# Delaying four weight loads, shortening the warm-up, summing weights by halves and preparing tile 2 earlier at the start of a convolution and joint kernel

## The chip, the cores and the metric

The kernel runs on one core of one Trainium2 chip. The metric is the time of one execution on the device in microseconds (us). Runs of one kernel spread by about half a per cent, so each kernel below was run five or six times, in rounds that alternate with the kernel before on the same chip. A ratio is the mean time of one kernel's fast runs over the mean of the other's fast runs of the same rounds. A difference within 2% counts as "same"; everything here lies inside that band, and the questions are about half per cents. PE is the matrix engine, VectorE (DVE) and ScalarE (ACT) do elementwise work, and PSUM is the memory that PE writes its sums to, `acc` in the profile. A hole is a stretch in which PE has to wait between two matmuls.

## The reference

Two convolutions over time with five taps (zero padding of two, stride two, gelu after each), then a projection, a tanh joint with a second input, and an output projection. Cut to what matters:

```
x: (2, 4000, 512)   w1, w2: (5, 512, 512)   g: (2, 8, 512)   w_f, w_g, w_o: (512, 512)
h = gelu(sum_i xp[:, i:i+T, :] @ w1[i])[:, ::2, :]
f = gelu(sum_i hp[:, i:i+T1, :] @ w2[i])[:, ::2, :]
j = tanh((f @ w_f)[:, :, None, :] + (g @ w_g)[:, None, :, :])
return j @ w_o                                   # (2, 1000, 8, 512), bf16
```

## The kernel before

A convolution tile is not computed as ten products (five taps, two output phases) but as seven, by a fast-filter scheme. It needs differences of the four input phases, called a0, b1, b3, a3, a1, a2 (the function `xf`, on VectorE, some of them after a copy called `shift` on ScalarE). It also needs sums of weights: 2(w1+w3), w0+w4-w2 and w0+w4+w2. After the seven products a `post` puts them together: ScalarE copies one PSUM bank to `cs`, VectorE makes two scaled sums and a third, and ScalarE applies gelu.

The first tile of 254 columns (`t0`) is special, because at the start neither the weight sums nor the transposed input exist. Its input comes by two plain loads, 512 rows of x each (`xr`), and PE transposes them. Output blocks m = 0, 1 are computed directly from the plain taps, one tap at a time (`direct`); blocks 2, 3 by the filter (`filt`). Everything else of x comes by transposing DMAs. Warm-up matmuls on zeros fill PE until the samples are there.

The parts that the change touches, with cuts:

```
NWARM = 12
...
for rt in range(2):
    load_xr(rt)                          # two plain sample loads, 512 KB each
for i in (0, 1, 3, 4, 2):
    load_w1("sp", i)                     # five taps, 512 KB each, same queue
for ph in (2, 3, 1, 0):
    load_x(0, ph, 272, 528)              # transposing DMAs, same queue
...
warm_mm(NWARM)
for pp in range(2):                      # pp 0: phases 0, 2; pp 1: phases 1, 3
    for rt in range(2):                  # the two sample loads
        ...16 transposes in all per rt; copy pp 0 on VectorE, pp 1 on ScalarE
...
def wsum04(wsb, wt, eng, m):             # a quarter (128 columns of outputs) at a time
    tt(eng, s, wsb[0, :, sl], wsb[4, :, sl], add)          # f32
    tt(eng, wt[0, :, sl], s, wsb[2, :, sl], sub)
    tt(eng, wt[2, :, sl], s, wsb[2, :, sl], add)
...
def post(self, m, where, vec=(), scal=()):
    act(c, ps.cols(C, n), ACT.Copy, scale=0.5)             # cs
    flush()                              # the pending gelu of the post before
    for f in scal: f()                   # shifts of the next tile
    ...two scalar_tensor_tensor on VectorE...
    for f in vec: f()                    # xf of the next tile
    tt("dve", tv, tv, ps.pair(A, step, n), add)
    pending.append(lambda: self.gelu(m, tv))
...
for w in ("a0", "b1", "b3", "a1"): t1.xf(w)
wsum04(w1_sb, w1_t, "dve", 0)
t1.xf("a2"); t1.xf("a3")
wsum04(w1_sb, w1_t, "dve", 1)
for m, A in base0.items():
    t0.post(m, (A, A + NT, A + NT + 256, 256))
...
if qi == 1:                              # tile 1's posts prepare tile 2
    vec  = [... (), ("a0",), ("b1", "b3"), ("a1", "a2", "a3") ...][m]
    scal = [... ("a0",), ("b1",), (), ("a3",) ...][m]
```

## Time and profile before

| | before |
|---|---|
| median time | 281.73 us at the time of the prediction (three runs, 280.79 to 282.26) |
| profiled run | 282.13 us, span 280.3 us |
| PE busy | 98% |
| first real matmul | 8.99 us |
| last real matmul starts | 276.87 us |

The page's first part gives each engine's busy time, its share of the span and its instructions (kernel before):

```profile
PE 273.9 (98%) x1436; PEld 137.8 (49%) x1436; DVE 188.0 (67%) x250; ACT 160.3 (57%) x191; POOL 30.2 (11%) x39
```

A PE that is 98% busy seems to leave nothing to gain. But warm-ups count as busy too. The timeline of PE shows where its time is not the kernel's work. Its columns are start, length, engine, line, operation, tiles, shape, count and, in brackets, idle time before it with what ended it (kernel before):

```profile
1.29 4.86 PE L298 MATMUL acc<-zero 128*128 128x512 bf16 x12 [1.29 <-POOL warm L284]
...
8.99 5.39 PE L298 MATMUL acc<-xs_49,w_sb 128*128 128x254 bf16 x48 [1.05 <-DMA w_sb<-in_w_dram]
...
35.54 1.85 PE L298 MATMUL acc<-xt_55,w_sb 128*128 128x500 bf16 x8
37.38 1.02 PE L298 MATMUL acc<-xs_50,w_sb 128*128 128x500 bf16 x4
38.24 1.01 PE L298 MATMUL acc<-xs_50,w_t 128*128 128x500 bf16 x4
39.71 1.02 PE L298 MATMUL acc<-xt_55,w_t 128*128 128x500 bf16 x4 [0.47 <-DVE xt_55 L287]
40.95 1.02 PE L298 MATMUL acc<-xs_50,w_t 128*128 128x500 bf16 x4 [0.22 <-DVE xs_50 L287]
42.15 1.00 PE L298 MATMUL acc<-xt_55,w_sb 128*128 128x500 bf16 x4 [0.18 <-DVE xt_55 L287]
```

PE waits for the first tap of w1 before 8.99 us, and it waits three times for VectorE's `xf` results of tile 2 near 40 us. The chain of work that ended last (start, length, what), near those holes (kernel before):

```profile
39.69 1.20 DVE xs_50 L287
40.89 1.12 DVE xt_55 L287
42.02 0.14 issue
42.15 234.13 PE acc L298 x1112
```

From 42.15 to 276.28 us it is PE alone. Before that the chain does not run through PE at all: after the first loads it goes through VectorE, with some stretches of ScalarE. VectorE's timeline shows one long wait, and ScalarE's shows its reason (kernel before):

```profile
26.12 0.75 DVE L499 SCALAR_TENSOR_TENSOR ty_67<-acc,cs_65 128x254 f32<-128x254 f32 x2
...
31.80 0.74 DVE L499 SCALAR_TENSOR_TENSOR ty_67<-acc,cs_66 128x246 f32<-128x246 f32 x2 [1.42 <-ACT cs_66 L291]
...
40.81 1.20 DVE L287 TENSOR_TENSOR xt_55<-xt_55,xs_50 128x2000 bf16<-128x2000 bf16 x1
...
29.00 0.68 ACT L291 ACTIVATE hT_61<-ty_68 128x508 bf16<-128x508 f32 x1 [0.44 <-DVE ty_68 L287]
29.57 1.86 ACT L291 ACTIVATE xt_55<-xs_50 128x2000 bf16<-128x2000 bf16 x1
31.33 0.37 ACT L291 ACTIVATE cs_66<-acc 128x246 f32<-128x246 f32 x1
```

ScalarE runs in order. A gelu waits for VectorE, a 1.86 us shift stands behind the gelu, and the short `cs` copy that VectorE wants stands behind the shift.

### The profile page before, as it was taken

The page shows a single profiled execution, that of the slowest core. Times are in us where ns is not written, and L with a number is a line of the kernel's source. Part 1 is how long each engine was busy: PE and PEld are TensorE (multiplying, and loading weights), DVE is VectorE, ACT ScalarE, POOL GpSimd, SP SyncE. Part 2 cuts the span into 40 slices and gives each one's busy share as a digit, 9 for nine tenths or more (in the row PEclk, how much of TensorE's full clock was granted, in tenths as well). Part 3 has the DMA queues.
Part 4 walks back from the last instruction along what each step waited for, and adds up shares of the span by engine and source line. Part 5 has one row for each costly group of instructions (what it writes and reads, how often), then busy time and mean ns, then how long its engine had stood idle before and what let it go on. Part 6 is the DMA issues. An engine that isn't in the chain of part 4 may idle for free.

```text
span 280.3 us, 3870 instructions
## 1 busy us (share of the span) xinstructions
PE 273.9 (98%) x1436; PEld 137.8 (49%) x1436; DVE 188.0 (67%) x250; ACT 160.3 (57%) x191; POOL 30.2 (11%) x39
## 2 busy tenths in 40 slices
PE   8899989999999999999999999999999999999995
PEld 3799934444444444444444444444444444444442
DVE  0989797956896766686424363676776775666764
ACT  2533949328426533932336565948957957966930
POOL 1000000099992000000000000000000000000000
PEclk9999999999999999999999999999999999999999
DMA  7999999990000000000000020444454445444444
GB/s 251 291 179 201 213 211 191 316 325 3 4 0 0 2 0 0 0 2 0 0 0 4 0 75 5 155 155 154 135 169 151 150 144 170 145 155 145 155 150 140
DMA packets 54719, 31.85 MB, mean 114 GB/s; under 512 B 31646, under 2 KB 54446, under 8 KB 54702
## 3 DMA queue, kind: packets, MB, share of 16 engines
q1 hardware_dynamic: 54702, 31.62, 41.8%
q8 instruction: 11, 0.18, 0.3%
q14 instruction: 6, 0.05, 0.1%
HBM read 7.86 MB, written 16.38 MB: 87 GB/s over the span
## 4 chain that ended last, share of the span: by engine, by line
PE 84%; SPq 6%; DVE 5%; issue 2%; ACT 1%; DMA 1%; DVEq 0%
PE acc L298 84%; SPq L330 4%; SPq L316 2%; DMA xs_49<-in_x_dram 1%; ACT xt_55 L291 1%; DVE xs_50 L287 1%; DVE xt_55 L287 1%; DVE w_t L287 1%; DVE ty_68 L499 1%; DVE ty_68 L287 0%; DVE xt_54 L287 0%; SPq L321 0%; DVE ty_67 L499 0%; DVE ty_69 L499 0%; DVE ssum_71 L287 0%
## 5 line engine op out<-in xcount | busy, mean ns | idle before, releaser
L298 PE MATMUL acc<-wo_sb,jT 128*128 128x512 bf16 (+1 forms) x504 | 108.3, 378 | 0.0
L298 PEld LDWEIGHTS acc<-wo_sb,jT 128*128 128x128 bf16 x504 | 49.3, 98 | 58.8
L298 PE MATMUL acc<-xt_55,w_sb 128*128 128x500 bf16 (+1 forms) x192 | 42.1, 357 | 0.2 <-DVE xt_55 L287 0.2
L291 ACT ACTIVATE jT<-feT_80,geT 128x1000 bf16<-128x1000 f32 (+6 forms) x44 | 35.8, 889 | 0.0
L291 ACT ACTIVATE jT<-feT_79,geT 128x1000 bf16<-128x1000 f32 (+4 forms) x40 | 35.1, 948 | 0.0
L298 PE MATMUL acc<-xt_54,w_sb 128*128 128x500 bf16 (+1 forms) x160 | 33.2, 342 | 0.0
L298 PEld LDWEIGHTS acc<-xt_55,w_sb 128*128 128x128 bf16 x192 | 18.6, 98 | 18.7 <-issue 0.9
L291 ACT ACTIVATE cs_65<-acc 128x500 f32<-128x500 f32 (+2 forms) x13 | 7.0, 538 | 27.3 <-PE acc L298 27.3
L298 PEld LDWEIGHTS acc<-xt_54,w_sb 128*128 128x128 bf16 x160 | 15.6, 98 | 13.0
L291 ACT ACTIVATE cs_66<-acc 128x500 f32<-128x500 f32 (+2 forms) x13 | 7.0, 536 | 21.8 <-PE acc L298 21.7
L298 PE MATMUL acc<-xs_49,w_sb 128*128 128x254 bf16 (+2 forms) x112 | 15.6, 286 | 1.1 <-DMA w_sb<-in_w_dram 1.1
L291 ACT ACTIVATE ost_93<-acc 128x512 bf16<-128x512 f32 x10 | 6.0, 597 | 16.4 <-PE acc L298 16.4
L679 DVE CAST ost_82<-acc 128x512 bf16<-128x512 f32 x11 | 7.6, 691 | 10.3 <-PE acc L298 10.3
L679 DVE CAST ost_88<-acc 128x512 bf16<-128x512 f32 x10 | 6.9, 692 | 10.3 <-PE acc L298 10.3
L298 PE MATMUL acc<-xs_49,w_t 128*128 128x246 bf16 (+2 forms) x72 | 13.8, 315 | 0.0
L287 DVE TENSOR_TENSOR ty_68<-ty_68,acc 128x1000 f32<-128x1000 f32 (+2 forms) x9 | 9.7, 1079 | 5.7 <-PE acc L298 5.7
L287 DVE TENSOR_TENSOR ty_67<-ty_67,acc 128x1000 f32<-128x1000 f32 (+2 forms) x9 | 9.7, 1078 | 5.1 <-PE acc L298 5.1
L298 PEld LDWEIGHTS acc<-xs_49,w_sb 128*128 128x128 bf16 x112 | 10.8, 97 | 4.0 <-DMA w_sb<-in_w_dram 1.2
L291 ACT ACTIVATE ost_87<-acc 128x512 bf16<-128x512 f32 x10 | 5.9, 593 | 11.4 <-PE acc L298 11.4
L287 DVE TENSOR_TENSOR ty_69<-ty_69,acc 128x1000 f32<-128x1000 f32 (+1 forms) x8 | 8.5, 1061 | 4.2 <-PE acc L298 4.1
L298 PE MATMUL acc<-xt_55,w_t 128*128 128x500 bf16 (+1 forms) x48 | 10.0, 341 | 0.5 <-DVE xt_55 L287 0.5
L679 DVE CAST ost_86<-acc 128x512 bf16<-128x512 f32 (+1 forms) x12 | 7.7, 646 | 2.6 <-PE acc L298 2.6
(116 smaller groups left out, 363.2 us busy)
## 6 DMA issues: line engine op xcount, KB each, us to landing
w_sb<-in_w_dram SPq DMA_DIRECT2D x10, 512.0 KB, 7.9
out_dram<-ost_82 SPq DMA_DIRECT2D x11, 128.0 KB, 1.9
out_dram<-ost_84 SPq DMA_DIRECT2D x10, 128.0 KB, 1.9
out_dram<-ost_86 SPq DMA_DIRECT2D x10, 128.0 KB, 1.9
out_dram<-ost_90 SPq DMA_DIRECT2D x10, 128.0 KB, 1.9
out_dram<-ost_83 SPq DMA_DIRECT2D x9, 128.0 KB
out_dram<-ost_85 SPq DMA_DIRECT2D x9, 128.0 KB
out_dram<-ost_87 SPq DMA_DIRECT2D x9, 128.0 KB
```

Of the source, the lines that this page charges most:

```text
L287: pl.op(eng, lambda e: e.tensor_tensor(out=o.ap, in0=a.ap, in1=b.ap, op=op), (a, b), (o,))
L291: pl.op("act", lambda e: e.activation(o.ap, i.ap, func, scale=scale, bias=0.0 if bias is None else bias.ap), rd, (o,))
L298: ins = e.matmul(o.ap, lhsT=l.ap, rhs=r.ap, start=start and n == 0, stop=stop and n == len(pairs) - 1, skip_group_check=not check)
L316: return pl.dma(eng, lambda e: e.dma_start(dst.ap, src), (), (dst,))
L330: pl.dma("sp", lambda e: e.dma_start_transpose(out=dst.ap, in_=src), (), (dst,))
L499: pl.op("dve", lambda e, o=o, f=f: e.scalar_tensor_tensor(out=o.ap, in0=d.ap, scalar=f, in1=c.ap, op0=ALU.mult, op1=add), (d, c), (o,))
L679: pl.op("dve", lambda e, o=o, v=v: e.tensor_copy(out=o.ap, in_=v.ap), (v,), (o,))
```

## The change

Its intent: let tap 0 land sooner, start PE sooner, take work and a wait off VectorE so that tile 2's operands are ready. The diff, cut to its core:

```diff
-    NWARM = 12
+    NWARM = 8
...
-        for i in (0, 1, 3, 4, 2):
-            load_w1("sp", i)
+        load_w1(0)
+        for i in (1, 3, 4, 2):
+            load_w1(i, xr_in[1])        # issued when the second sample load has landed
...
-        for pp in range(2):
-            for rt in range(2):
+        for rt in range(2):
+            for pp in range(2):
...
+            warm_mm(1 + rt)
...
-            if which == "a0" and keep: tt("dve", o(0), src[2, :, off-1:off-1+n], ph(2), sub)
                                         # t0's a0 now: a shift on ScalarE, then xf
...  wsum13: the doubling moves from VectorE to ScalarE
...
+        def w1sums(h, part):            # half of the outputs; part "s": w0+w4 kept in f32,
+            ...                         # "+": s + w2, "-": s - w2
...
-        wsum04(w1_sb, w1_t, "dve", 2)
-        wsum04(w1_sb, w1_t, "dve", 3)
+        w1sums(1, "s")
...     tile 1's xf, with w1sums(0, "s"), (1, "+"), (1, "-"), (0, "+"), (0, "-") between them
...
             def post(...):
                 act(c, ps.cols(C, n), ACT.Copy, scale=0.5)
+                for f in first:
+                    f()
                 flush()
...
-            t0.post(m, (A, A + NT, A + NT + 256, 256))
+            t0.post(m, (...), (), (), (lambda: tiles[2].shift("a0"),) if m == 2 else ())
+        tiles[2].xf("a0")
...
-   vec  = [..., (), ("a0",), ("b1", "b3"), ("a1", "a2", "a3")][m]
-   scal = [..., ("a0",), ("b1",), (), ("a3",)][m]
+   vec   = [..., (), ("b1",), ("b3",), ()][m]
+   first = [..., ("b1",), (), ("a3",), ()][m]
+   if m == 3:
+       for w in ("a1", "a2", "a3"): nx.xf(w)      # ahead of the last post
```

Below, "the hold" is the late issue of taps 1 to 4; "the head" is the hold, the eight warm-ups and the new transpose order together; "the sums" are the half sums with the doubling and the extra shift on ScalarE; "the posts" are the reordered posts.

More of the change, by code (lines that the diff above doesn't have):

```diff
@@ L264, in bass_standalone__seq2seq_rnn_t_joint__speech_kernel @@
         ty = [at(f"ty{i}", [2, NT], FP32) for i in range(3)]
-        ssum = [at(f"ssum{i}", [NK, P], FP32) for i in range(2)]
+        ssum = at("ssum", [NK, P], FP32)
         geT = at("geT", [NK * BU], FP32)
@@ L332, in bass_standalone__seq2seq_rnn_t_joint__speech_kernel, with load_w1 @@
         act(warm[0:1], warm[1:2], ACT.Gelu_apprx_tanh)
-        for rt in range(2):
-            load_xr(rt)
-        def load_w1(eng, i):
-            load_w(eng, w1_sb[i], w1[i].rearrange("(k c) d -> c k d", c=P))
-        for i in (0, 1, 3, 4, 2):
-            load_w1("sp", i)
+        xr_in = [load_xr(rt) for rt in range(2)]
+        def load_w1(i, after=None):
+            o = load_w("sp", w1_sb[i], w1[i].rearrange("(k c) d -> c k d", c=P))
+            if after is not None:
+                o.deps[("dma", after.idx)] = True
+        load_w1(0)
+        for i in (1, 3, 4, 2):
+            load_w1(i, xr_in[1])
         for ph in (2, 3, 1, 0):
@@ L354, in bass_standalone__seq2seq_rnn_t_joint__speech_kernel @@
         psb = ps.h[:, :].bitcast(BF16)
-        for pp in range(2):
-            for rt in range(2):
+        for rt in range(2):
+            for pp in range(2):
                 bk = 4 + 2 * pp + rt
@@ L383, in xf @@
             h = NT // 2
-            if which == "a0" and keep:
-                tt("dve", o(0), src[2, :, off - 1:off - 1 + n], ph(2), sub)
-            elif which == "b3" and keep:
+            if which == "b3" and keep:
                 tt("dve", dst[0, :, h:h + n], ph(3), ph(1), sub)
@@ L422, in wsum13 @@
             tt(eng, v, wsb[1, :, lo:hi], wsb[3, :, lo:hi], add)
-            pl.op(eng, lambda e: e.tensor_scalar(out=v.ap, in0=v.ap, scalar1=2.0, scalar2=None, op0=ALU.mult), (v,), (v,))
+            if eng == "dve":
+                act(v, v, ACT.Copy, scale=2.0)
+            else:
+                pl.op(eng, lambda e: e.tensor_scalar(out=v.ap, in0=v.ap, scalar1=2.0, scalar2=None, op0=ALU.mult), (v,), (v,))
+        def w1sums(h, part):
+            sl = slice(h * 2 * P, (h + 1) * 2 * P)
+            s = ty[h][:].map(lambda a: a.rearrange("p s c -> p (s c)").rearrange("p (k c) -> p k c", k=NK))
+            if part == "s":
+                tt("dve", s, w1_sb[0, :, sl], w1_sb[4, :, sl], add)
+            elif part == "+":
+                tt("dve", w1_t[2, :, sl], s, w1_sb[2, :, sl], add)
+            else:
+                tt("dve", w1_t[0, :, sl], s, w1_sb[2, :, sl], sub)
         def wsum04(wsb, wt, eng, m):
             sl = slice(m * P, (m + 1) * P)
-            s = ssum[m % 2][:]
+            s = ssum[:]
             tt(eng, s, wsb[0, :, sl], wsb[4, :, sl], add)
             tt(eng, wt[0, :, sl], s, wsb[2, :, sl], sub)
-            tt(eng, wt[2, :, sl] if wsb is w1_sb else wsb[2, :, sl], s, wsb[2, :, sl], add)
+            tt(eng, wsb[2, :, sl], s, wsb[2, :, sl], add)
         count = {"unit": 0}
@@ L484, in gelu, with post @@
                 act(o, src, ACT.Gelu_apprx_tanh)
-            def post(self, m, where, vec=(), scal=()):
+            def post(self, m, where, vec=(), scal=(), first=()):
                 A, C, Dd, step = where
@@ L541, in filt @@
                     t0.product(w, m, o, w in ("a0", "b2"))
-        for w in ("a0", "a1", "a2", "b3"):
-            t0.xf(w)
-        for w in ("b1", "a3"):
+        for w in ("a0", "b1", "a3"):
             t0.shift(w)
+        for w in ("a1", "a2", "b3", "a0", "b1", "a3"):
             t0.xf(w)
         wsum13(w1_sb, w1_t, "dve")
-        wsum04(w1_sb, w1_t, "dve", 2)
-        wsum04(w1_sb, w1_t, "dve", 3)
+        w1sums(1, "s")
         for i in (0, 1, 3):
@@ L556, in bass_standalone__seq2seq_rnn_t_joint__speech_kernel @@
         direct(2)
-        filt("b2", "a1", "a2")
         for b in range(B):
@@ L563, in bass_standalone__seq2seq_rnn_t_joint__speech_kernel @@
             t1.shift(w)
-        for w in ("a0", "b1", "b3", "a1"):
+        w1sums(0, "s")
+        w1sums(1, "+")
+        w1sums(1, "-")
+        t1.xf("a0")
+        w1sums(0, "+")
+        for w in ("b1", "b3"):
             t1.xf(w)
-        wsum04(w1_sb, w1_t, "dve", 0)
-        t1.xf("a2")
-        t1.xf("a3")
-        wsum04(w1_sb, w1_t, "dve", 1)
+        w1sums(0, "-")
+        for w in ("a1", "a2", "a3"):
+            t1.xf(w)
+        filt("b2", "a1", "a2")
         for m in (0, 1):
@@ L572, in bass_standalone__seq2seq_rnn_t_joint__speech_kernel @@
         for m, A in base0.items():
-            t0.post(m, (A, A + NT, A + NT + 256, 256))
+            t0.post(m, (A, A + NT, A + NT + 256, 256), (), (),
+                    (lambda: tiles[2].shift("a0"),) if m == 2 else ())
+        tiles[2].xf("a0")
         def load_rest():
@@ L629, in bass_standalone__seq2seq_rnn_t_joint__speech_kernel @@
                 where = tile.products(m, *((LATE0,) if qi < 3 and m == 0 else ()))
-                vec, scal = [], []
+                vec, scal, first = [], [], []
                 if qi == 1:
-                    vec = [lambda w=w: nx.xf(w) for w in ((), ("a0",), ("b1", "b3"), ("a1", "a2", "a3"))[m]]
-                    scal = [lambda w=w: nx.shift(w) for w in (("a0",), ("b1",), (), ("a3",))[m]]
+                    vec = [lambda w=w: nx.xf(w) for w in ((), ("b1",), ("b3",), ())[m]]
+                    first = [lambda w=w: nx.shift(w) for w in (("b1",), (), ("a3",), ())[m]]
+                    if m == 3:
+                        for w in ("a1", "a2", "a3"):
+                            nx.xf(w)
                 elif nx:
@@ L636, in bass_standalone__seq2seq_rnn_t_joint__speech_kernel @@
                     scal = [lambda w=w: nx.shift(w) for w in (("a0", "b1"), ("a3",), (), ())[m]]
-                tile.post(m, where, vec, scal)
+                tile.post(m, where, vec, scal, first)
                 if qi == 3:
```

## The prediction

> **What bounds the kernel now.** The page gives PE busy 273.9 of 280.3 us. In PE's timeline the real matmuls start at 8.99 us and run back to back at full granted clock (128x254 every 0.109 us), with only three holes, 0.47, 0.22 and 0.18 us, between 39 and 42.2 us. The chain of waits is PE alone from 42.15 to 276.3 us. So only the first 42 us can change: at most the 9 us head and 0.87 us of holes.
>
> The head: twelve warm-up matmuls from 1.29 to 5.99 us (0.427 us apart until the clock rises at 5.57 us, which agrees with the Trainium skill, "TensorE: Matmul & The Clock Gate", "The HAM clock gate": 1.2 GHz until about 3.4 us of activity), transposes to 7.8 us; tap 0's samples are copied by 7.93 us. PE then idles 1.05 us for tap 0 of w1. That landed at 8.95 us although the samples had landed by 5.27 us and each later tap took about 1.45 us: its landing parts show most queues done by 6.9 us and two late. The holes end on xf results of VectorE, nearly full from 18 to 42 us.
>
> **What the change does.**
> 1. Taps 1 to 4 are issued only after 5.27 us. Tap 0 has the queues to itself: estimate 6.5 to 7 us. Tap 1: first bytes follow an issue by 1.05 us (first sample load), estimate landed 7.9 to 8.5 us; PE wants it 1.74 us after its start, so in time.
> 2. Four warm-ups fewer (-1.7 us, cold), three short ones added. Transposes start at 4.7 us, partly at the low clock; done near 7.1 us, tap 0's samples copied near 7.5 us. New start: about 7.6 us instead of 8.99, bound by transposes and copies.
> 3. VectorE: twelve f32 sums of 512 columns (0.61 us apart, 7.3 us) become six of 1024 (estimate 1.1 us each, from the 1000-column f32 add of 1.08 us: 6.6 us; f32 gets no fast mode, as the skill's "VectorE: DVE Perf Modes", tier table, says and these times agree). The doubling (0.61 us) goes to ScalarE (estimate 1.9 us, from a 2000-column copy), idle there for 5.6 us. One extra ScalarE shift, 1.0 us. More sums precede the x transposes' landing, filling VectorE's wait.
> 4. Tile 2's shifts and xf move ahead of gelu, so VectorE's 1.42 us wait for cs (behind a 1.87 us shift on ScalarE) should go; tile 2's xf end near 38 us, PE wants the last near 39.3 us. The holes go.
>
> Nothing after 42 us changes.
>
> **Sum.** 1.4 us (start) plus 0.9 us (holes) = 2.3 us from the profiled run of 282.13: 279.8. I say **279.9 us, range 278.7 to 281.3**. Faster by over 2% would need 5.6 us, which the head does not hold: 0.02. Within 2%: 0.96. Slower by over 2%: 0.02.
>
> **What would show it.** First real matmul at 7.2 to 8.0 us; w1's first landing under 7.2 us, PE's wait for it under 0.3 us; no PE wait over 0.1 us between 20 and 45 us; VectorE's first post near 24 us (was 26.12).
>
> **What would make it wrong.** A late queue still holds tap 0 to 9 us (only the holes are gained, about 281). Tap 1 lands after 9.4 us and PE stalls. The clock rises later. The x transposes are issued about 1.4 us later and land later, so tile 2's shift on ScalarE, now in front of tile 0's second post, waits for its phase (23.04 us before) and delays cs and VectorE; holes of up to 1 us reappear near 38 us. Each costs back about 1 us or less; together, equal to before.

## The result, and the profile after

| | before | after |
|---|---|---|
| median time, six runs each | 281.71 us | 279.94 us |
| lowest to highest | 280.79 to 282.26 | 279.92 to 280.91 |
| ratio of fast runs, 95% interval | | 0.9949 (0.9927 to 0.9972) |
| profiled run | 282.13 us | 280.62 us |
| first real matmul | 8.99 us | 8.31 us |
| last real matmul starts | 276.87 us | 275.37 us |

The total came out as predicted. The parts did not. PE's busy time is practically unchanged, as the page shows (kernel after):

```profile
PE 273.8 (98%) x1435; PEld 138.8 (50%) x1435; DVE 188.1 (67%) x243; ACT 163.2 (59%) x193; POOL 30.9 (11%) x39
```

PE's timeline (kernel after):

```profile
1.30 3.59 PE L298 MATMUL acc<-zero 128*128 128x512 bf16 x8 [1.30 <-POOL warm L284]
4.68 1.91 PE L365 MATMUL acc<-ident,xr_63 128*128 128x128 bf16 x16
6.39 0.63 PE L298 MATMUL acc<-zero 128*128 128x512 bf16 x1
6.82 1.11 PE L365 MATMUL acc<-ident,xr_64 128*128 128x128 bf16 x16
...
8.31 1.90 PE L298 MATMUL acc<-xs_49,w_sb 128*128 128x254 bf16 x16
10.78 3.65 PE L298 MATMUL acc<-xs_49,w_sb 128*128 128x254 bf16 x32 [0.57 <-DMA w_sb<-in_w_dram]
...
35.59 1.85 PE L298 MATMUL acc<-xt_55,w_sb 128*128 128x500 bf16 x8
...
40.65 1.01 PE L298 MATMUL acc<-xt_55,w_sb 128*128 128x500 bf16 x4
```

The first matmul on tap 0 is 0.68 us earlier, but then PE waits for tap 1. Tile 2 begins at 35.59 us, against 35.54 before: by then the whole lead of the new head is gone, before the holes have been reached. The matmul that began at 42.15 us before begins at 40.65 us, and that 1.50 us is the whole difference of the two profiles. In this pair of profiles all of it was won between 35.5 and 42 us.

A hole is larger than the idle time that is printed before it, because the modelled end of a matmul overlaps the start of the next. Measured by starts, in the undisturbed stream a 128x254 matmul follows its predecessor by 0.109 us and a 128x500 one by about 0.21 us. In the kernel before, the steps into 37.38, 39.71, 40.95 and 42.15 us were 0.367, 0.843, 0.594 and 0.557 us; less 0.21 each, that is 1.52 us, against 0.87 us of printed idle time. In the kernel after, the step into 10.78 us was 0.843 us, 0.73 us too long, though 0.57 us are printed.

The chain now has no VectorE in it between the first loads and the last output copy (kernel after):

```profile
1.17 4.11 DMA xr_64<-in_x_dram
...
5.30 5.44 DMA w_sb<-in_w_dram
...
10.78 264.00 PE acc L298 x1368
```

It passes through the hold: the second sample load lands at 5.28 us, tap 1 is issued then, lands at 10.74 us, and PE runs from there. On VectorE the wait of 1.42 us is gone and the last `xf` of tile 2 ends 3.8 us earlier (kernel after; VectorE's lines first, then ScalarE's):

```profile
24.34 0.74 DVE L517 SCALAR_TENSOR_TENSOR ty_67<-acc,cs_65 128x254 f32<-128x254 f32 x2
...
26.09 0.75 DVE L517 SCALAR_TENSOR_TENSOR ty_68<-acc,cs_66 128x254 f32<-128x254 f32 x2 [0.29 <-ACT cs_66 L291]
...
37.01 1.19 DVE L287 TENSOR_TENSOR xt_55<-xt_55,xs_50 128x2000 bf16<-128x2000 bf16 x1
...
23.57 0.38 ACT L291 ACTIVATE cs_65<-acc 128x254 f32<-128x254 f32 x1 [0.54 <-PE acc L298]
23.85 1.86 ACT L291 ACTIVATE xt_55<-xs_50 128x2000 bf16<-128x2000 bf16 x1
25.61 0.37 ACT L291 ACTIVATE cs_66<-acc 128x254 f32<-128x254 f32 x1
```

### The profile page after: what moved, and what is told of

Its sections match the earlier page's. It is cut to its first block, busy times and chain, and to the rows that moved or that the text cites. A ratio compares the mean times of both kernels' runs of the same rounds, so it can differ in the third digit from the quotient of the medians.

```text
span 278.8 us, 3866 instructions
## 1 busy us (share of the span) xinstructions
PE 273.8 (98%) x1435; PEld 138.8 (50%) x1435; DVE 188.1 (67%) x243; ACT 163.2 (59%) x193; POOL 30.9 (11%) x39
## 4 chain that ended last, share of the span: by engine, by line
PE 95%; DMA 3%; issue 0%; DVE 0%; SPq 0%; DVEq 0%
PE acc L298 95%; DMA w_sb<-in_w_dram 2%; DMA xr_64<-in_x_dram 1%; DVE ost_85 L704 0%; SPq L321 0%; DVEq L238 0%; DVE ost_84 L704 0%
```

## The experiments

Theory A, formed from the two traces: the kernel before is bound by VectorE up to the last `xf` of tile 2, and PE by its own start only when VectorE is in time. Theory B, which is closer to the prediction: most of the gain comes from the head. For each kernel the profile gives the tap landings, the end of the copies of tap 0's samples, the first real matmul and the end of tile 2's last `xf`. They are gathered here, with every run; all times but the ratios are in us, and those of the profile are of one run.

| kernel | tap 0 lands | copies end | first real matmul | tap 1 lands | last xf of tile 2 ends | profiled run | median | ratio to before (95%) |
|---|---|---|---|---|---|---|---|---|
| before | 8.95 | 7.93 | 8.99 | 10.42 | 42.01 | 282.13 | 281.71 | 1 |
| after | 7.62 | 8.21 | 8.31 | 10.74 | 38.20 | 280.62 | 279.94 | 0.9949 (0.9927 to 0.9972) |
| hold_only | 7.50 | 7.20 | 7.54 | 11.00 | 42.64 | 282.74 | 282.33 | 1.0030 (1.0007 to 1.0052) |
| vec_only | (low clock) | | | | | 487.24 | 280.10 | 0.9949 (0.9927 to 0.9971) |
| no_hold | 7.61 | 7.84 | 7.94 | 9.12 | 37.11 | 279.48 | 280.00 | 0.9948 (0.9931 to 0.9965) |
| old_head | 7.12 | 7.23 | 7.33 | 9.32 | 37.27 | 279.18 | 280.65 | 0.9967 (0.9944 to 0.9990) |
| posts_only | 7.56 | 7.67 | 7.77 | 9.06 | 38.43 | 279.33 | 279.48 | 0.9929 (0.9914 to 0.9943) |
| sums_only | 8.45 | 7.49 | 8.49 | 9.93 | 39.93 | 280.09 | 280.03 | 0.9956 (0.9938 to 0.9975) |
| fast_head | 8.45 | 7.31 | 8.49 | 9.95 | 37.66 | 280.05 | 279.70 | 0.9940 (0.9921 to 0.9959) |
| fast_head_hold0 | 7.67 | 7.50 | 7.72 | 9.17 | 36.88 | 279.28 | 279.28 | 0.9916 (0.9903 to 0.9929) |
| slack4 | 7.29 | 8.17 | 8.27 | 10.01 | 42.35 | 282.97 | 282.71 | 1.0043 (1.0025 to 1.0060) |
| after_again | 7.01 | 7.13 | 7.24 | 9.45 | 37.22 | 279.31 | 280.10 | 0.9944 (0.9926 to 0.9963) |
| lean | 7.08 | 7.68 | 7.78 | 8.94 | 38.77 | 279.38 | 279.19 | 0.9917 (0.9905 to 0.9929) |
| lean_half | 6.14 (half) | 7.55 | 7.65 | 8.10 | 38.12 | 279.28 | 279.73 | 0.9938 (0.9924 to 0.9953) |

All gave correct results. Two relations hold through the table. First, the first real matmul comes within 0.11 us of the later of tap 0's landing and the copies' end, in every row with profile times. Second, where there are no holes, the time of the profiled run is the first real matmul, plus what tap 1 costs, plus 266.3 us from the first real matmul's start to the last one's, plus about 5.2 us. For no_hold, 7.94 + 266.3 + 5.2 is 279.4, measured 279.48; for after, 8.31 + 0.73 + 266.3 + 5.2 is 280.5, measured 280.62.

### hold_only: the hold alone

```diff
 (kernel before)
-        for i in (0, 1, 3, 4, 2):
-            load_w1("sp", i)
+        load_w1(0)
+        for i in (1, 3, 4, 2):
+            load_w1(i, xr_in[1])
```

> The kernel before, with nothing changed but that taps 1 to 4 of w1 are issued after the second plain sample load has landed. Theory A (head and VectorE must both move: PE's lead is eaten by the holes on xf results as long as VectorE still ends tile 2's xf near 42 us): first real matmul near 8.0 us instead of 8.99, but the holes near 38 to 42 us grow by about as much, so the time stays within 0.3 us of before. Theory B (the gain of the change is tap 0's earlier landing): 0.7 to 1.0 us faster than before, holes as large as before.

Measured: 282.33 us, ratio 1.0030. Tap 0 landed at 7.50 us, PE started 1.45 us earlier than before, and the kernel was slower, by about 0.8 us. Neither theory had expected that. PE's timeline of this kernel:

```profile
7.54 1.92 PE L298 MATMUL acc<-xs,w_sb 128*128 128x254 bf16 x16 [0.33 <-DMA w_sb<-in_w_dram]
11.05 3.65 PE L298 MATMUL acc<-xs,w_sb 128*128 128x254 bf16 x32 [1.59 <-DMA w_sb<-in_w_dram]
...
40.35 1.02 PE L298 MATMUL acc<-xt,w_t 128*128 128x500 bf16 x4 [0.47 <-DVE xt L287]
41.59 1.02 PE L298 MATMUL acc<-xs,w_t 128*128 128x500 bf16 x4 [0.22 <-DVE xs L287]
42.79 1.00 PE L298 MATMUL acc<-xt,w_sb 128*128 128x500 bf16 x4 [0.18 <-DVE xt L287]
```

The early start is lost to tap 1 at once: the step into 11.05 us was 1.860 us, 1.75 us too long, which is 0.30 us more than was won. The three holes stand where they stood, moved by 0.64 us, since the last `xf` ends 0.63 us later. VectorE is late because the hold delays its first weight sum too: w1+w3 waits for tap 3, which landed at 12.43 us instead of 11.94 (kernel before, then hold_only):

```profile
12.13 1.22 DVE L287 TENSOR_TENSOR w_t<-w_sb 128x2048 bf16<-128x2048 bf16 x1
12.53 1.23 DVE L287 TENSOR_TENSOR w_t<-w_sb 128x2048 bf16<-128x2048 bf16 x1 [1.05 <-DMA w_sb<-in_w_dram]
```

That is 0.40 us of the 0.65 us by which the first post is later (26.77 us); VectorE's later waits make the rest. In its chain the last stretch of PE alone is as long as before to the hundredth:

```profile
42.79 234.13 PE acc L298 x1112
```

So before and hold_only both last as long as VectorE's end at tile 2 plus a constant. That refutes B's forecast: the hold on top of the old VectorE order is worth nothing. It does not test the other half of A, that PE's lead is lost at the holes, because tap 1 had already eaten the lead. By the starts the holes grew only from 1.52 to 1.85 us, which is the 0.63 us that VectorE was later less the 0.3 us that PE was later. No run joined a faster head that has no wait for tap 1 to the old VectorE order.

### vec_only: the change without its head

```diff
 (kernel after)
-    NWARM = 8
+    NWARM = 12
...  transposes in their old order, no warm-ups between them, all five taps issued at once
```

> The change without its head: twelve warm-up matmuls, old order of the transposes, all five taps issued at once; only the half sums, the doubling on ScalarE, the extra shift and the reordered posts are kept. Theory A: first real matmul near 9.0 us as before, no holes after 20 us, about 1.5 us faster than before (0.9945 to 0.996 of it). Theory B: within 0.5 us of before.

Measured: ratio 0.9949, the same as the full change, from five runs. The sixth, the profiled one, took 487.24 us: the granted clock stayed low throughout, at 0.56 on average, and it is left out. (The median of 280.10 us in the table still counts it; that of the five runs is 279.73 us.) So the whole gain is had without the head, as far as intervals of about 0.6 us to each side can tell, which is what A says. Where this kernel's PE started in its fast runs could not be read.

### no_hold: the change without the hold

```diff
 (kernel after)
-        load_w1(0)
-        for i in (1, 3, 4, 2):
-            load_w1(i, xr_in[1])
+        for i in (0, 1, 3, 4, 2):
+            load_w1("sp", i)
```

> The changed kernel with the hold on taps 1 to 4 taken away, warm-ups and transposes as changed. If tap 0's landing sets the start: tap 0 lands near 9 us again, first real matmul near 9.0 us, no wait for tap 1, 0.7 us slower than the changed kernel in its usual runs (279.93), so about 280.6. Rival (copies set the start and the hold is worth nothing, or costs because of the late tap 1): within 0.3 us of the changed kernel or faster.

Measured: 280.00 us, ratio 0.9948. The rival was right: a worth of the hold does not show in time, with intervals of about 0.5 us to each side. In this profile tap 0 landed at 7.61 us although nothing was held, and tap 1 at 9.12 us, in time for PE, with no wait for it.

### old_head: the hold with twelve warm-ups and the old transposes

```diff
 (kernel after)
-    NWARM = 8
+    NWARM = 12
...  transposes in their old order, no warm-ups between them
```

> The changed kernel with twelve warm-ups and the old order of transposes, hold kept. If the eight warm-ups help (transposes 1.3 us earlier): slower than the changed kernel by 0.3 us or more. Rival (the transposes run at the low clock behind eight warm-ups, so their end does not move; tap 0's copies end at 7.93 us with twelve and 8.21 with eight): first real matmul near 8.0 us and the same time as the changed kernel or up to 0.3 us less.

Measured: median 280.65 us, ratio 0.9967 with an interval that overlaps that of the full change. The profiled run, at 279.18 us, was the fastest of its six, so its start at 7.33 us is not typical. Inconclusive: it neither shows a use of the eight warm-ups nor excludes one of 0.5 us.

### posts_only and sums_only: each half of the VectorE part alone

posts_only is the kernel before with the `post` part of the diff (its `first` argument, tile 2's a0 ahead, the three last `xf` ahead of the last post) and nothing else. sums_only is vec_only with that part undone.

> The kernel before with only the reordered posts (tile 2's shifts ahead of the gelu, its last three xf ahead of the last post): quarter sums, doubling on VectorE, warm-ups, transposes and loads as before. Theory A (what matters is only whether VectorE ends tile 2's xf before PE asks for the last of them, about 32.3 us after the first real matmul): xf end near 39.7 us instead of 42.0, no holes, and the whole gain of the VectorE part, 0.994 to 0.9965 of before, though half of that part is missing. Rival (each half of the VectorE part is worth its own share): about 0.9975.

> The kernel before with only the sums part (half sums with kept partial sums, doubling on ScalarE, the a0 shift on ScalarE, sums moved ahead of tile 1's xf); posts in their old order, head and loads as before. Theory A: first post near 24.3 us instead of 26.1, xf end near 40.3 us, in time for PE: no holes, again 0.994 to 0.9965 of before. Rival (shares add): about 0.9975; or, if the cs wait grows by what the sums save, xf end still near 42 us and the time as before.

Measured: posts_only 279.48 us, ratio 0.9929 (faster than either theory's range, though its interval, 0.9914 to 0.9943, reaches A's); sums_only 280.03 us, ratio 0.9956. Neither profile has a hole after 20 us. The shares do not add: either half alone brings the last `xf` in time, and the other half then buys nothing. They do it in different ways. posts_only loses the `cs` wait; sums_only keeps a 1.42 us `cs` wait, but its first post starts at 24.05 us instead of 26.12. VectorE's first post and last `xf` of posts_only, then the first post, the wait and the last `xf` of sums_only:

```profile
24.95 0.74 DVE L501 SCALAR_TENSOR_TENSOR ty<-acc,cs 128x254 f32<-128x254 f32 x2
...
37.23 1.19 DVE L287 TENSOR_TENSOR xt<-xt,xs 128x2000 bf16<-128x2000 bf16 x1
...
24.05 0.75 DVE L514 SCALAR_TENSOR_TENSOR ty<-acc,cs 128x254 f32<-128x254 f32 x2
...
29.73 0.73 DVE L514 SCALAR_TENSOR_TENSOR ty<-acc,cs 128x246 f32<-128x246 f32 x2 [1.42 <-ACT cs L291]
...
38.73 1.19 DVE L287 TENSOR_TENSOR xt<-xt,xs 128x2000 bf16<-128x2000 bf16 x1
```

The first post of posts_only also starts 1.17 us earlier than in the profile of before, though nothing ahead of it was changed. In this run the loads landed earlier (tap 3 at 10.58 us instead of 11.94) and VectorE waited less. So of the 3.58 us by which its last `xf` is earlier, about 1.2 us are not the edit; one profile against one cannot size a part.

The expectation of posts_only had PE ask for the last operand 32.3 us after its start. That number came from the profile of after and contains the 0.73 us for tap 1; the right one is 31.6 us (40.65 - 8.31 - 0.73). With it, sums_only had only 0.2 us to spare (8.49 + 31.6 = 40.1, `xf` end 39.93) and posts_only 0.9 us (7.77 + 31.6 = 39.4, `xf` end 38.43). So sums_only cannot use a start much earlier than 8.3 us, which may be why it is the slower of the two; that is an argument, not a test.

### fast_head and fast_head_hold0: what sets the start

```diff
 (kernel after; fast_head also without the hold)
-    NWARM = 8
+    NWARM = 6
-            warm_mm(1 + rt)
 (fast_head_hold0 alone)
-            load_w1(i, xr_in[1])
+            load_w1(i, xr_in[0])        # held until the first sample load has landed
```

> The changed kernel without the hold, with six warm-ups instead of eight and none between or after the transposes, so that the transposes of the first half start when its samples land (4.05 us) and those of the second follow at once. With no holes left the time is the first real matmul plus 266.3 us of PE plus about 5.2 us. If copies set the start: tap 0's copies end by 7.4 us even at the low clock, 0.4 to 0.6 us faster than without the hold alone (280.0). If tap 0's landing sets it (7.6 to 9 us without the hold): no faster than that run.

> The same quick head with taps 1 to 4 held only until the first sample load has landed (about 4.05 us) instead of the second (5.3 us). Tap 0 should land by 7.1 to 7.6 us and tap 1 at 9 to 9.5 us, in time for PE; first real matmul near 7.5 us, no wait for tap 1: 279.2 us or less, the fastest of all. If a late queue still holds tap 0 or tap 1, it is not faster than the quick head without any hold.

Measured: fast_head 279.70 us, ratio 0.9940; in its profile the copies ended at 7.31 us but tap 0 landed at 8.45 us, and the start was 8.49 us. With the copies out of the way, tap 0 set the start. fast_head_hold0: 279.28 us, ratio 0.9916, from 278.86 to 279.40 over five runs; no wait for tap 1. Its start, 7.72 us, was set by tap 0 at 7.67 us, a little late for what was expected. Its interval does not overlap that of no_hold, though they ran in different rounds on different chips, each against the kernel before.

### slack4: VectorE slowed on purpose

```diff
 (kernel after, before tile 0's first post)
+        for _ in range(4):
+            tt("dve", <half of ty[2], unused there>, w1_sb[0, :, 0:2 * P], w1_sb[4, :, 0:2 * P], add)
```

> The changed kernel with four useless f32 sums of 1024 columns (1.14 us apart, 4.5 us) put on VectorE just before tile 0's first post; nothing else differs. Theory A: the changed kernel has about 2.4 us to spare there (xf end 38.2 us, PE wants the last at 40.65 us), so 1.6 to 2.2 us are lost and holes on xf results are back near 41 us: about 281.8 us. Rival 1 (VectorE's work counts one to one): 284.4 us. Rival 2 (VectorE is off the path, the gain came from elsewhere): 280 us.

Measured: 282.71 us, which is 2.6 us over after_again (280.10 us) of the same rounds. Both rivals are refuted: 4.5 us of useless VectorE work costs more than nothing and less than 4.5 us. The expected 1.6 to 2.2 us was too little. Who PE waited for, from 24 to 46 us (total, times, longest; kernel slack4):

```profile
PE acc L298 <- DVE xs L287: 0.9, 1, 0.9
PE acc L298 <- DVE ty L517: 0.6, 1, 0.6
PE acc L298 <- DVE ty L287: 0.3, 1, 0.3
PE acc L298 <- issue: 0.3, 1, 0.3
PE acc L298 <- DVE xt L287: 0.2, 1, 0.2
```

The expectation looked at the last `xf` alone. PE also waited for PSUM that a post frees (the two `ty` lines) and for b3 (the `xs` line), which came before it. The matmuls from first to last took 269.44 us here, against 266.3 us without holes, so 3.1 us in the profiled run.

### after_again: the changed kernel once more

No edit.

> The changed kernel once more, unaltered, beside the others on one chip: 279.9 to 280.6 us, and a second profile of it. If the late tap 1 of the first profile was its rule: a wait of 0.5 us or more for tap 1 again. If it was chance: none, and the time is the first real matmul plus 266.3 us plus about 5.3 us.

Measured: 280.10 us, ratio 0.9944, from 279.31 to 281.01. In its profile PE started at 7.24 us, and the step into tap 1's first matmul was 0.634 us, 0.53 us too long. The clock had risen at 4.68 us, where it rose at 6.92 us in the first profile, and the copies ended at 7.13 us instead of 8.21. So both profiles of this kernel show a wait for tap 1, while the start moves by 1.07 us with the clock. Here no part of tap 1 was late (all sixteen landed between 8.95 and 9.45 us); the load, issued at 5.39 us, was as a whole too late for a PE that wanted it at 8.98 us.

### lean and lean_half: a smaller change

```diff
 (kernel before)
+  the posts, as in posts_only
-    NWARM = 12
+    NWARM = 6
+  transposes by sample load, no warm-ups between them
-        for i in (0, 1, 3, 4, 2):
-            load_w1("sp", i)
+        load_w1(0)
+        for i in (1, 3, 4, 2):
+            load_w1(i, xr_in[0])
 (lean_half instead)
+        load_w1(0, columns 0 to 256); then, held on xr_in[0]: 1, 3, the rest of 0, 4, 2
```

> The kernel before with only the reordered posts, six warm-ups, transposes ordered by sample half, and taps 1 to 4 held until the first sample load has landed; sums and doubling as before. Theory A: half sums are not needed, VectorE ends tile 2's xf near 38.5 us against PE's need near 40 us; no holes; first real matmul near 7.5 us: 279.2 us, equal to the quick head with the half sums and faster than the changed kernel by 0.5 us or more.

> The same, but only the half of tap 0 that the first matmuls read (256 of 512 columns) leaves at once; its other half goes behind taps 1 and 3. If tap 0's landing sets the start: it lands 0.5 us or more earlier, the start falls to the copies' end (7.3 to 7.5 us) in every run, 278.8 us and a narrower spread. If a late queue is chance and not a matter of bytes: no faster than the run with the whole tap.

Measured: lean 279.19 us, from 279.13 to 279.50 over five runs, ratio 0.9917. It has quarter sums, the doubling on VectorE and no extra shift, and it matches fast_head_hold0. Beside it, on the same chip, the full change took 280.10 us with a ratio of 0.9944 (0.9926 to 0.9963); lean's interval (0.9905 to 0.9929) overlaps that by a hair, so lean is faster by its medians, by 0.9 us, and not quite clear by the intervals. Its interval overlaps that of posts_only (0.9914 to 0.9943, on another chip) as well, so these runs do not show that lean's head adds anything to the posts alone. In its profile there is no hole; the last line is the products that read the last `xf`, which began at 42.15 us before:

```profile
1.29 2.74 PE L298 MATMUL acc<-zero 128*128 128x512 bf16 x6 [1.29 <-POOL warm L284]
4.21 3.19 PE L365 MATMUL acc<-ident,xr 128*128 128x128 bf16 x32 [0.18 <-DMA xr<-in_x_dram]
7.78 5.41 PE L298 MATMUL acc<-xs,w_sb 128*128 128x254 bf16 x48 [0.38 <-issue]
...
39.42 1.01 PE L298 MATMUL acc<-xt,w_sb 128*128 128x500 bf16 x4
```

lean_half missed: 279.73 us, no narrower and no faster. In its profile half a tap landed at 6.14 us, but the clock rose only at 7.23 us, the copies ended at 7.55 us and set the start at 7.65 us. That run took 279.28 us; what its slower runs (up to 280.25 us) waited for is not known.

## Why the prediction was right or wrong

The time was right: 279.94 us against 279.9, and partly by luck. Two terms of the sum were wrong in opposite directions, the start by 1.4 us too much and the holes by 0.6 us too little, so that they cancelled only in part: the two profiled runs differ by 1.51 us, the medians by 1.77 us, and not by 2.3 us. The rest of the match comes from the run that the prediction counted from, which at 282.13 us lay 0.4 us above the median.

- **The start.** "1.4 us (start)" was the failing step. In the profile PE began 0.68 us earlier and then lost 0.73 us to tap 1: a net gain of nothing in this profile. (It is of one of the slower runs, 280.62 us. For a run of 279.93 us, as four of the six were, the sum under the table leaves about 8.4 us for start and tap 1 together instead of 9.04; this is an estimate. But vec_only, without the head, is as fast.) The step "PE wants it 1.74 us after its start, so in time" is where it broke. The estimate had tap 1 landed at 7.9 to 8.5 us; it landed at 10.74. The parts of its landing in the trace show two errors. Even the first part came at 8.64 us, after the estimate, and fourteen of sixteen were there by 9.13 us; the last two came at 10.55 and 10.74. The first error alone makes PE wait when it starts early, as in after_again; here it was the two late parts, since PE wanted the tap at 10.05 us. The Trainium skill, "DMA: Bandwidth & Descriptors", "Why a DMA increments its semaphore by 16 and not by 1", says that each participating DMA engine adds its own part; the trace agrees, and a load is as late as its slowest part. The prediction had seen that for tap 0 and did not carry it to tap 1. It did name the risk: "Tap 1 lands after 9.4 us and PE stalls".
- **What bound the start.** The step "bound by transposes and copies" was right: copies at 8.21 us, tap 0 at 7.62. The size was off because the clock rose at 6.92 us and not at 5.57 as in the profile before: with this head the copies ended at 7.13, 7.84 and 8.21 us where it rose at 4.68, 6.14 and 6.92 us (after_again, no_hold, after). The Trainium skill, "TensorE: Matmul & The Clock Gate", "The HAM clock gate", says that the window "doesn't reset when your kernel starts"; the runs agree. With twelve warm-ups, the first at 1.29 us in each, the clock rose at 4.09, 4.15, 4.69, 5.04 and 5.57 us, with eight at 4.68, 6.14 and 6.92 us (as far as the traces record the rise, and without vec_only). One profile's rise must not be taken for a constant.
- **The holes.** "0.9 us (holes)" had the right mechanism and too small a size. It added the printed idle times; by the starts of the matmuls the holes cost 1.52 us. This is the term that carried the result, and vec_only, posts_only and sums_only show it without the head.
- **VectorE.** First post at 24.34 us (predicted near 24), `xf` end at 38.20 us (near 38), half sums 1.14 us apart (estimate 1.1), the doubling 1.91 us on ScalarE (estimate 1.9), no PE wait between 20 and 45 us: all right. The tier table of the Trainium skill, "VectorE: DVE Perf Modes", "The perf-mode tier table", which gives a bf16 `tensor_tensor` twice the speed of an f32 one, agrees again: an f32 sum of 1024 columns took 1.14 us to the next one, a bf16 difference of 2000 columns 1.12 us.
- **Credit.** The prediction gave steps 3 and 4 one hole term together and did not see that either alone would do. posts_only and sums_only show that.
- **Unresolved.** Why one or two parts of a load come late, and in which runs, is open. With the hold on the second sample load, tap 0 landed at 7.01 to 7.62 us in five profiles; without any hold, leaving out the run at the low clock, at 7.56 to 8.95 us in five. So in these profiles the hold brings tap 0 forward, as the change intended, but what it gains there it gives back at tap 1: the start plus the wait for tap 1 is 8.41 us in the mean of the five with it and 8.34 us of the five without. Whether the eight warm-ups help is open too.

## What to carry to other kernels

When the chain of work runs through another engine between PE's start and the point from which PE runs alone, first ask what an earlier start of PE can be worth while that engine is late. Here the chain of the kernel before says that it is worth nothing, but no run tested that cleanly. Once that engine is in time, further relief of it is worth nothing, as vec_only beside posts_only shows. Test each part of a change alone, since parts that clear the same deadline do not add. Size holes by the distance between starts, not by printed idle time, and ask of every load that is put behind another when each of its readers, on every engine, wants its slowest part: the hold cost PE at tap 1 and VectorE at tap 3.

## What the Trainium skill lacked or had wrong

- "TensorE: Matmul & The Clock Gate", "The HAM clock gate": it speaks of a clock seen stuck at a quarter for over 50 us. In one of six runs of vec_only the record of the granted clock stays at 0.555 from 4.27 us to the end, its first 128x254 matmuls followed each other by about 0.20 us instead of 0.109, and the run took 487.24 us beside 279.40 to 280.63 us of the other five. A single run with a PE that is busy all the time can thus stay low from end to end, and a timing of one run can be wrong by three quarters.
- "DMA: Bandwidth & Descriptors", "Latency and other measured facts": it says that DMA engines 7 and 15 are usually slower than the others, and gives as its best guess a cause that lies in DMAs issued from GpSimd; it does not say by how much. All loads here are issued from SyncE. In the changed kernel fourteen parts of a 512 KB load landed within 0.5 us (8.64 to 9.13 us) and the last two 1.4 and 1.6 us later, and a load queued behind it on the same queue again had two late parts (12.23 and 12.41 us). It is not so in every run: in old_head and after_again all parts of tap 1 landed within 0.3 and 0.5 us. Whether these are the same two engines the records here do not tell.
- No page that I read tells that the idle time before a matmul understates a hole: 0.87 us were printed where the starts of the matmuls show 1.52 us.
